# Sharing out the hidden layer of a relative-position bias anew, with the order of a head pair's steps changed

## The chip, the core and the metric

The kernel runs on one core of one Trainium2 chip. A core has TensorE (matrix products into the accumulator memory PSUM), VectorE, ScalarE and GpSimd (element work; GpSimd reads and writes only the core's main memory SBUF here) and SyncE, whose queue SP issues most DMAs. Each engine takes its instructions in order from a queue of its own and waits on semaphores for the others. The metric is the device time of one execution in microseconds (us), median over several runs.

## The reference

Attention with a learned bias of the relative position, then two gated feed-forward stages. Two batches, 8 heads, 576 positions, head size 64; the hidden layer of the bias has 32 units.

```python
scores = scale * np.matmul(q, k.transpose(0, 1, 3, 2))
psi_rel = np.log1p(np.abs(rel))                       # rel[i, j] = i - j
psi_i = np.log1p(np.maximum(pos[:, None], 1.0))
h = np.maximum((psi_rel / psi_i)[..., None] @ w1 + b1, 0.0)
scores = scores + (h @ w2).transpose(2, 0, 1)[None]   # one bias for both batches
attn = np.exp(scores - np.max(scores, axis=-1, keepdims=True))
attn = attn / (np.sum(attn, axis=-1, keepdims=True) + 1e-09)
x = np.matmul(attn, v)                                # then x @ w_a * (x @ w_b) @ w_out,
                                                      # and a softmax-gated, normed stage
```

## The kernel before

**The bias rows.** The bias of 16 query rows (one T; 576 / 16 = 36 of them) is made in three steps. `bias_hidden(T)` (line 348) makes four relus: for each quarter qd a tile h of 128 partitions (4 rows times 32 hidden units) by 576 positions, read as a shifted window of one table `tabs`, plus a column, then the maximum with 0. The division by psi_i is left until the end, which the maximum allows. Which engine makes each of the four is a string of `HIDDEN` (line 29): v is VectorE, p GpSimd (both line 365), a ScalarE (line 363). The strings are taken by T modulo their number, from the first tuple for the first 128 query rows (T = 0 to 7) and from the last for all others. `bias_sums(T)` (line 368) multiplies the four h by w2 on TensorE, 16 instructions (line 373) into four bands of one PSUM tile bps. `bias_out(T)` (line 376) copies bps, scaled, to a tile st with ScalarE (line 383) and sends st by DMA on SP into the rows of the bias (line 385).

**The prelude** (lines 514 to 535): T = 0 to 8. In step T come the relus of T, then sums and rows of T - 1, then the subtraction of one piece of turned queries or keys and the transposes and high copy of the next: a piece is transposed by TensorE (line 275), its rounded high part is copied by ScalarE (line 308) and the remainder is subtracted by VectorE (lines 313 and 317). Loads for the second query unit, the second batch's keys and the values are issued on SP behind the last rows.

**The loop** (lines 605 to 666) runs over 36 head pairs, 9 units of 128 query rows (`units`) by 4 pairs of heads, and three more steps that empty the pipeline. In step m:

- `scores` (line 389) of both heads of pair m; each head takes a PSUM tile from the pool `ps_s`, which has two buffers and also serves bps. The second head's buffer, `spare`, takes also the tails of the transposed shares of pair m - 2 (line 439) and four transposes of queries for the next unit (line 275).
- `biased` (line 405): VectorE adds the bias and takes the minimum of the (negated) scores in one pass for each head (line 415); `powers` (line 419): ScalarE's exponential with its sum (line 422).
- `kept_tails` and `high`: ScalarE copies tails (line 455) and the high part of the new queries (line 308) out of `spare`; `lower` (line 310): VectorE subtracts for the low part (line 317).
- `turned` (line 441): TensorE transposes the shares of pair m - 2 (line 450) into the one buffer of `ps_t`; `kept` (line 458) copies one half of the result with VectorE (r = 1) and one with ScalarE (r = 0) (line 464).
- `values` (line 466): shares of pair m - 3 times values, 40 small products on TensorE (line 482). At the last pair of a unit, `inputs_high` and `inputs_low` (lines 488 and 493) split the finished outputs with ScalarE and VectorE.
- In steps 0 to 26: `bias_sums` and `bias_out` of T = m + 9, and `bias_hidden` of T + 1 (before the change its VectorE relus come ahead of `lower`, the others at the end).
- `summed_powers` (line 424): GpSimd adds 1e-9 to the sums (line 427), VectorE takes the reciprocal (line 428); `shares` (line 430): GpSimd multiplies each head's exponentials by it (line 433).
- `others`: work for later stages (loads of values, and from step 27 on the first weights), keyed by twice the step. In steps 1 to 3 the second batch's keys are turned as pieces; in the last two pairs of a unit the queries of the unit after next are fetched on SP (line 256).

The text of the program is the order of every engine's queue: nothing is rearranged. Buffers of a pool are given to tiles when the program is built, and a tile's first writer waits for the readers of the tile that had its buffer.

**Behind the loop** come the feed-forward stages, bound by TensorE; they reuse the memory of the attention and begin when it ends.

Of the kernel before, what the change touches and what calls it, by code (L numbers as in the profile page):

```python
# [25 lines left out]

LAG = 2

HIDDEN = (("vpva", "vpvp"), ("vpvp",))

LOADS = ((0, 1), (1, 1), (2, 2), (3, 2))
FIRST = ((-7, -5, -3, 1, 2, 3), (-6, -4, -2, 3, 4, 5), (-5, 0, 2, 5, 6, 7), (2, 4, 5, 6, 8, 9))
# [18 lines left out]
def tile_kernel(ctx, tc, q, k, v, w1, b1, w2, w_a, w_b, w_out, w_in2, w_out2, g_ln, psi, rpsi, out):  # L51
# [19 lines left out]
    scale = 1.0 / math.sqrt(D)  # L71
# [88 lines left out]
    with ExitStack() as actx:  # L160
# [149 lines left out]
        def lower(views, by=1.0):  # L310
            for hi, lo, ps in views:
                if by == 1.0:
                    nc.vector.tensor_tensor(out=lo, in0=ps, in1=hi.bitcast(F32), op=ALU.subtract)
                    continue
                parts_ = [(lo, ps, hi)] if len(ps.shape) == 3 else [(lo[:, h], ps[:, h], hi[:, h]) for h in range(2)]
                for l_, p_, h_ in parts_:
                    nc.vector.scalar_tensor_tensor(out=l_, in0=p_, scalar=by, in1=h_.bitcast(F32), op0=ALU.mult, op1=ALU.subtract)
# [30 lines left out]
        def bias_hidden(T, engines="vpa"):  # L348

            it, r, c = place(T)  # L350
            kinds = HIDDEN[min(it, len(HIDDEN) - 1)]
            kinds = kinds[T % len(kinds)]
            hs = bias_w.setdefault(T, [None] * 4)
            for qd in range(4):
                e = kinds[qd]
                if e not in engines:
                    continue
                t0 = it * P + r + 16 * qd
                h = hp.tile([P, S], F32, tag="h", name=f"h_{T}_{qd}")
                win = tb[:, OFF - t0 - c:OFF - t0 - c + S]  # L360
                sc = nb[:, c, t0 // 16:t0 // 16 + 1]
                if e == "a":
                    nc.scalar.activation(h, win, AF.Relu, bias=sc)
                else:
                    (nc.vector if e == "v" else nc.gpsimd).tensor_scalar(h, win, sc, 0.0, op0=ALU.add, op1=ALU.max)  # L365
                hs[qd] = h
# [38 lines left out]
        def biased(u, h):  # L405

            it, _ = units[u]
            ps = st_.pop(("s", u, h))
            if h % 2 == 0:
                st_["e", u, h // 2] = ep.tile([P, 2 * S], F32, tag="e", name=f"e_{u}_{h}")  # L410
            e2 = st_["e", u, h // 2]
            e = e2[:, (h % 2) * S:(h % 2 + 1) * S]
            nm = sp.tile([P, 1], F32, tag="nm", name=f"nm_{u}_{h}")
            halves = lambda a: a.rearrange("p (a j) -> p a j", a=2)
            nc.vector.tensor_tensor_reduce(out=halves(e), in0=ps[:, :, 0:SH], in1=halves(bias_t[it][:, h, :]), op0=ALU.add, op1=ALU.min,  # L415
                                           scale=1.0, scalar=3.0e38, accum_out=nm)
            st_[u, h] = e, nm

        def powers(u, h):
            e, nm = st_[u, h]  # L420
            sums, _ = st_[u]
            nc.scalar.activation(e, e, AF.Exp, bias=nm, scale=-1.0, accum_out=sums[:, h:h + 1])  # L422

        def summed_powers(u, p):
            sums, rec = st_[u]
            heads = slice(2 * p, 2 * p + 2)
            nc.gpsimd.tensor_scalar(rec[:, heads], sums[:, heads], 1e-9, 1.0, op0=ALU.add, op1=ALU.mult)  # L427
            nc.vector.reciprocal(rec[:, heads], rec[:, heads])  # L428

        def shares(u, h):  # L430
            e, _ = st_.pop((u, h))
            _, rec = st_[u]
            nc.gpsimd.tensor_scalar(e, e, rec[:, h:h + 1], 1.0, op0=ALU.mult, op1=ALU.mult)  # L433
# [7 lines left out]
        def turned(u, p):  # L441

            e2 = st_.pop(("e", u, p))
            pt = ps_t.tile([P, 2, 512], F32, tag="t", name=f"pt_{u}_{p}")
            for j in range(2):
                for c in range(NC):
                    at = (j * NC + c) * HF
                    cols = j * S + j * TL + c * P
                    for r, rows in enumerate(ROWS):
                        nc.tensor.transpose(pt[:, r, at:at + HF], e2[rows, cols:cols + P], ident[rows, rows])  # L450
            st_["pt", u, p] = pt
# [6 lines left out]
        def kept(u, p, r):  # L458

            if r == 1:  # L460
                st_["et", u, p] = etp.tile([P, 2 * NC, P], F32, tag="et", name=f"et_{u}_{p}")
            dst = st_["et", u, p][:, :, ROWS[r]]
            pt = st_["pt", u, p][:, r].rearrange("p (c t) -> p c t", t=HF)
            (nc.vector.tensor_copy if r else nc.scalar.copy)(dst, pt)

        def values(u, p):

            it, bs = units[u]
            if p == 0:
                st_["x", u] = ps_x.tile([P, HP, P], F32, tag="x", name=f"px_{u}")  # L470
            px = st_["x", u]
            et, ett = st_.pop(("et", u, p)), st_.pop(("ett", u, p))
            n = P // len(bs)
            for c in range(NC + 1):
                for j, part in ((j, part) for j in range(2) for part in range(2)):

                    rows = slice(j * D + part * HID, j * D + (part + 1) * HID)
                    for m, b in enumerate(bs):
                        cols = slice(m * n, (m + 1) * n)
                        lhsT = (vsb[:, b, c] if c < NC else vtl[:, b])[:, p, j, part * HID:(part + 1) * HID]  # L480
                        rhs = et[:, j * NC + c, cols] if c < NC else ett[:, cols]
                        nc.tensor.matmul(px[rows, p, cols], lhsT, rhs, start=(c == 0 and m == 0), stop=(c == NC), skip_group_check=True)  # L482
# [14 lines left out]
        pairs = [(u, p) for u in range(NU) for p in range(HP)]  # L497
# [101 lines left out]
        def others(n):  # L599
            for f, args in extra.pop(n, []):  # L600
                f(*args)

        bias_hidden(sums_at[0])
        NP = len(pairs)
        for m in range(NP + LAG + 1):
            now = pairs[m] if m < NP else None
            up = pairs[m - LAG] if 0 <= m - LAG < NP else None
            out_ = pairs[m - LAG - 1] if 0 <= m - LAG - 1 < NP else None
            T, after = sums_at.get(m), sums_at.get(m + 1)
            views = []  # L610
            if now:
                u, p = now
                scores(u, 2 * p)
                spare = scores(u, 2 * p + 1)
                if (u, p) in ((NU - 3, HP - 1), (NU - 2, 1)):
                    clear_q(NU - 1, NU - 2 - u == 0)
            elif up:
                spare = ps_s.tile([P, 2, 512], F32, tag="s", name=f"tails_{m}")
            if up:
                turned_tails(*up, spare)  # L620
            if now and u + 1 < NU:
                g, i = divmod(p, 2)
                nat = fetched[("q", u + 1, g, 0)]
                turn(spare, QUERIES, nat, (2 * i, 2 * i + 1))
                views = q_views(u + 1, g, i, spare, QUERIES)
            if now:
                biased(u, 2 * p)
                powers(u, 2 * p)
                biased(u, 2 * p + 1)
            if up:  # L630
                kept_tails(*up, spare)
            high(views, -scale)
            if now:
                powers(u, 2 * p + 1)
            if up:
                turned(*up)
            if T is not None:
                bias_sums(T)
            if out_:
                values(*out_)  # L640
            if up:
                kept(*up, 1)
            others(2 * m)
            if after is not None:
                bias_hidden(after, "v")
            lower(views, -scale)
            if T is not None:
                bias_out(T)
            if up:
                kept(*up, 0)  # L650
            if after is not None:
                bias_hidden(after, "pa")
            for w in keys_at.get(m, []):
                made = piece(w)
                high(*made)
                lower(*made)
            if now:
                summed_powers(u, p)
                shares(u, 2 * p)
                shares(u, 2 * p + 1)  # L660
            if out_ and out_[1] == HP - 1:
                inputs_high(out_[0])
                inputs_low(out_[0])
            if now and p > 1 and u + 2 < NU:
                fetch(("q", u + 2, p - 2, 0))
            others(2 * m + 1)
# [155 lines left out]
    up = ctx.enter_context(tc.tile_pool(name="up", bufs=2))  # L822
# [117 lines left out]
    for i, u in enumerate(seq[:-2]):  # L940
        after = seq[i + 2]
# [66 lines left out]
```

## Time and profile before

| | us |
|---|---|
| median of 3 runs | 610.28 (608.60 to 612.89) |
| the profiled execution | 612.79 |
| its span, first to last instruction | 611.0 |
| prelude (first relu to first scores) | 6.3 to 41.6 |
| pairs 0 to 3 | 41.6 to 70.5 |
| pairs 4 to 26, with bias rows | 70.5 to 217.4 |
| pairs 27 on, to the end of the attention | 217.4 to 281.9 |
| feed-forward stages | 281.9 to 611.0 |

The profile is of one execution. Times in a row are us from the span's start; an instruction is named by its line, engine, operation and its tiles (output <- inputs, numbers left out). PE is TensorE, PEld its weight load, DVE is VectorE, ACT ScalarE, POOL GpSimd. In brackets stands how long the engine had been idle ahead of it and what ended that.

### The profile page before, as it was taken

Reading aid. Unit: us, or ns where it says so; the run is one execution under the profiler, and the core shown is the slowest. Engines: PE = TensorE matmul, PEld = TensorE weight load, DVE = VectorE, ACT = ScalarE, POOL = GpSimd, SP = SyncE. Lnnn points to the kernel's source line nnn. Section 1 sums busy time; section 2 is a strip of 40 time slices with the busy share of each in tenths; the row PEclk is TensorE's granted clock in tenths of the full one; section 3 lists DMA queues with packets and bytes.
Section 4 is the critical chain, followed back from the end, with each engine's and each line's share of the span. In section 5 each row is a group of like instructions: output and inputs, shape, how many; then the busy total and the mean of one; then the engine's idle time right before and its main releaser. Section 6 shows DMA issues by size and latency. Waiting matters only on the chain.

```text
span 611.0 us, 13442 instructions
## 1 busy us (share of the span) xinstructions
PE 527.6 (86%) x5416; PEld 458.6 (75%) x5416; DVE 396.5 (65%) x846; ACT 263.7 (43%) x584; POOL 288.4 (47%) x276
## 2 busy tenths in 40 slices
PE   7767766766667778889899999999999999999997
PEld 2324554555546667789899999999999998888887
DVE  4426646556556457753887998988988556675562
ACT  3425544545545456532555543444244432321221
POOL 6998899999999954410322221223412433000000
PEclk9996899899988989989899999999999999999999
DMA  5239733233132451104435443434531000000001
GB/s 134 77 88 192 165 75 77 58 77 75 46 88 59 114 142 59 38 1 138 141 112 165 138 138 121 151 111 137 160 115 36 2 0 1 18 35 18 17 18 52
DMA packets 63521, 51.75 MB, mean 85 GB/s; under 512 B 41182, under 2 KB 53731, under 8 KB 63460
## 3 DMA queue, kind: packets, MB, share of 16 engines
q1 hardware_dynamic: 63184, 50.88, 30.7%
q8 instruction: 42, 0.69, 0.5%
q14 instruction: 19, 0.16, 0.1%
q10 hardware_dynamic: 276, 0.02, 0.0%
HBM read 36.73 MB, written 2.36 MB: 64 GB/s over the span
## 4 chain that ended last, share of the span: by engine, by line
PE 60%; POOL 27%; issue 4%; DVE 3%; ACT 3%; DMA 3%; SPq 1%; POOLq 0%; DVEq 0%; ACTq 0%
PE pm L128 24%; POOL h L365 20%; PE po L128 12%; PE py L905 8%; PE ph L845 8%; POOL e L433 6%; PE bps L373 2%; PE px L482 1%; DMA nat_q<-in_q_dram 1%; PE pl L886 1%; ACT e L422 1%; PE s L401 1%; DMA words<-in_moe_w_out_dram 1%; POOL rec L427 1%; DVE e L415 1%
## 5 line engine op out<-in xcount | busy, mean ns | idle before, releaser
L365 POOL TENSOR_SCALAR h<-tabs 128x576 f32<-128x576 f32 x68 | 152.1, 2250 | 2.2 <-DVE tabs L216 2.2
L98 POOL TENSOR_SCALAR f<-f 128x512 f32<-128x512 f32 x48 | 41.3, 860 | 146.9 <-ACT f L94 140.2
L373 PE MATMUL bps<-h,w2bd 128*32 128x288 f32 x576 | 61.6, 459 | 46.8 <-DVE nm L415 39.2
L422 ACT ACTIVATE e<-e,nm 128x576 f32<-128x576 f32 x72 | 55.8, 775 | 91.8 <-DVE nm L415 90.3
L128 PE MATMUL pm<-xhi,abh 128*128 128x384 f32 x240 | 80.2, 334 | 0.0
L128 PE MATMUL pm<-xhi,abl 128*128 128x384 f32 x240 | 80.2, 334 | 0.0
L128 PE MATMUL pm<-xlo,abh 128*128 128x384 f32 x240 | 80.2, 334 | 0.0
L373 PEld LDWEIGHTS bps<-h,w2bd 128*32 128x32 f32 x576 | 22.6, 118 | 69.1 <-DVE nm L415 42.3
L415 DVE CUSTOM_DVE_ANT_0 e<-s,bias 128x576 f32<-128x576 f32 x72 | 51.9, 753 | 17.3 <-PE s L401 8.9
L433 POOL TENSOR_SCALAR e<-e,rec 128x576 f32<-128x576 f32 x72 | 55.2, 779 | 13.9 <-DVE rec L428 12.3
L128 PE MATMUL po<-gh,oh 128*128 128x384 f32 x144 | 48.5, 337 | 0.6 <-DVE x2s L776 0.6
L428 DVE RECIPROCAL rec<-rec 128x2 f32<-128x2 f32 x36 | 6.0, 166 | 65.8 <-POOL rec L427 65.5
L128 PE MATMUL po<-gh,ol 128*128 128x384 f32 x144 | 48.4, 336 | 0.0
L128 PE MATMUL po<-gl,oh 128*128 128x384 f32 x144 | 48.4, 336 | 0.0
L128 PEld LDWEIGHTS pm<-xhi,abl 128*128 128x128 f32 x240 | 45.1, 188 | 0.0
L128 PEld LDWEIGHTS pm<-xhi,abh 128*128 128x128 f32 x240 | 45.1, 188 | 0.0
L128 PEld LDWEIGHTS pm<-xlo,abh 128*128 128x128 f32 x240 | 45.1, 188 | 0.0
L872 POOL TENSOR_TENSOR small<-small,mhalf 128x1 f32<-128x1 f32 x9 | 5.0, 552 | 83.0 <-DVE small L871 49.4
L110 DVE SCALAR_TENSOR_TENSOR f<-words,f 128x512 int32<-128x512 int32 x48 | 42.5, 885 | 1.6
L482 PE MATMUL px<-et,vsb 128*32 128x128 f32 (+1 forms) x1280 | 43.5, 281 | 0.0
L482 PEld LDWEIGHTS px<-et,vsb 128*32 128x32 f32 x1280 | 37.4, 118 | 6.4 <-issue 1.5
L147 ACT COPY one<-pm 128x384 f32<-128x384 f32 x36 | 17.2, 477 | 56.7 <-PE pm L128 56.7
(149 smaller groups left out, 1282.6 us busy)
## 6 DMA issues: line engine op xcount, KB each, us to landing
bias<-st SPq DMA_DIRECT2D x40, 288.0 KB, 3.5
words<-in_moe_w_out_dram SPq DMA_DIRECT2D x20, 512.0 KB, 3.7
words<-in_moe_w_a_dram SPq DMA_DIRECT2D x12, 512.0 KB, 3.6
words<-in_moe_w_b_dram SPq DMA_DIRECT2D x12, 512.0 KB, 3.6
nat_q<-in_q_dram SPq DMA_DIRECT2D x32, 128.0 KB, 3.5
words<-in_moe_w_in_dram SPq DMA_DIRECT2D x8, 512.0 KB, 3.6
arena<-in_k_dram SPq DMA_DIRECT2D x16, 128.0 KB, 3.2
vsb<-in_v_dram SPq DMA_DIRECT2D x16, 128.0 KB, 2.8
```

The lines of the kernel that those rows point to most:

```text
L98: engine.tensor_scalar(f, f, WORD_MAX, WORD_MIN, op0=ALU.min, op1=ALU.max)
L110: nc.vector.scalar_tensor_tensor(out=b, in0=words[:, :, 0], scalar=29, in1=b, op0=ALU.logical_shift_right, op1=ALU.bitwise_or)
L128: nc.tensor.matmul(ps, w, x, start=(i == 0), stop=(i == n - 1))
L147: nc.scalar.copy(one, ps[:, 1])
L365: (nc.vector if e == "v" else nc.gpsimd).tensor_scalar(h, win, sc, 0.0, op0=ALU.add, op1=ALU.max)
L373: nc.tensor.matmul(bps[32 * qd:32 * qd + 32, a, 0:SH], w2bd, h[:, a * SH:(a + 1) * SH], start=True, stop=True)
L415: nc.vector.tensor_tensor_reduce(out=halves(e), in0=ps[:, :, 0:SH], in1=halves(bias_t[it][:, h, :]), op0=ALU.add, op1=ALU.min, scale=1.0, ...
L422: nc.scalar.activation(e, e, AF.Exp, bias=nm, scale=-1.0, accum_out=sums[:, h:h + 1])
L433: nc.gpsimd.tensor_scalar(e, e, rec[:, h:h + 1], 1.0, op0=ALU.mult, op1=ALU.mult)
L482: nc.tensor.matmul(px[rows, p, cols], lhsT, rhs, start=(c == 0 and m == 0), stop=(c == NC), skip_group_check=True)
L845: nc.tensor.matmul(ph[u][:, a], x[:, kc, cols], w[:, kc, a * 512:(a + 1) * 512], start=(i == 0), stop=(i == 3 * KD - 1))
L905: nc.tensor.matmul(ps, x[:, c, :], w[:, c, cols], start=(i == 0), stop=(i == 3 * KF - 1))
```

## The change

Three things. `HIDDEN` has one tuple of four strings for all T: of 16 relus 10 are VectorE's and 3 each ScalarE's and GpSimd's (before: 8 and 8 on VectorE and GpSimd in the loop; in the first 8 T, ScalarE also made one in every second T). The quarter that GpSimd makes is always the first. The sum, the reciprocal and the shares of a pair are issued one step later, the first two behind the next pair's `biased`, the shares behind its second `powers`. And within a step `values` comes ahead of `bias_sums`, both `kept` and `lower` ahead of `bias_hidden`, all of whose relus now stand together ahead of `bias_out`.

```diff
-HIDDEN = (("vpva", "vpvp"), ("vpvp",))
+HIDDEN = (("pvav", "vvav", "pvva", "pvvv"),)
...
         for m in range(NP + LAG + 1):
             now = pairs[m] if m < NP else None
+            last = pairs[m - 1] if 0 < m <= NP else None
...
                 biased(u, 2 * p)
                 powers(u, 2 * p)
                 biased(u, 2 * p + 1)
+            if last:
+                summed_powers(*last)
             if up:
                 kept_tails(*up, spare)
             high(views, -scale)
             if now:
                 powers(u, 2 * p + 1)
+            if last:
+                for h in range(2):
+                    shares(last[0], 2 * last[1] + h)
             if up:
                 turned(*up)
+            if out_:
+                values(*out_)
             if T is not None:
                 bias_sums(T)
-            if out_:
-                values(*out_)
             if up:
                 kept(*up, 1)
+                kept(*up, 0)
+            lower(views, -scale)
             others(2 * m)
             if after is not None:
-                bias_hidden(after, "v")
-            lower(views, -scale)
+                bias_hidden(after)
             if T is not None:
                 bias_out(T)
-            if up:
-                kept(*up, 0)
-            if after is not None:
-                bias_hidden(after, "pa")
             for w in keys_at.get(m, []):
                 made = piece(w)
                 high(*made)
                 lower(*made)
-            if now:
-                summed_powers(u, p)
-                shares(u, 2 * p)
-                shares(u, 2 * p + 1)
```

## Rows read from the trace of the kernel before

**Rows 1.** The page's chain that ended last: shares of the span by line

```profile
PE pm L128 24%; POOL h L365 20%; PE po L128 12%; PE py L905 8%; PE ph L845 8%; POOL e L433 6%; PE bps L373 2%; PE px L482 1%; DMA nat_q<-in_q_dram 1%; PE pl L886 1%; ACT e L422 1%; PE s L401 1%; DMA words<-in_moe_w_out_dram 1%; POOL rec L427 1%; DVE e L415 1%
```

**Rows 2.** By stage: us; busy PE, PEld, DVE, ACT, POOL (count); clock; DMA share; GB/s

```profile
6.30:41.60 35.30, 27.85 (x212) 11.48 (x212) 16.18 (x34) 12.29 (x22) 35.08 (x17) 1.00 0.40 100
41.60:70.50 28.90, 19.30 (x241) 13.36 (x242) 15.83 (x41) 14.73 (x33) 24.19 (x19) 0.76 0.82 175
70.50:217.40 146.90, 99.00 (x2080) 80.06 (x2076) 83.67 (x234) 75.21 (x189) 136.81 (x115) 0.95 0.34 77
217.40:281.90 64.50, 54.54 (x1089) 48.68 (x1088) 39.70 (x95) 32.92 (x86) 23.14 (x38) 0.92 0.19 52
```

**Rows 3.** The chain in order of time, one round of it: start, us, what

```profile
124.32 1.46 POOL e L433 x2
125.78 4.37 POOL h L365 x2
```

**Rows 4.** Timeline of TensorE: first scores of pair 4 and of pair 27

```profile
70.52 0.38 PE L401 MATMUL s<-khi,qhi 64*128 64x288 f32 x2
...
217.35 0.40 PE L401 MATMUL s<-khi,qhi 64*128 64x288 f32 x2
```

**Rows 5.** Waits from 70.5 to 217.4: us in total, times, longest

```profile
DVE rec L428 <- POOL rec L427: 61.2, 23, 2.8
...
PEld s L401 <- ACT st L383: 11.3, 15, 0.8
```

**Rows 6.** Durations, ns (minimum/median/maximum), by line; the last a mean in the loop

```profile
L365 DVE TENSOR_SCALAR h<-tabs x72: 501/514/1001, 6.3 to 210.5; 128x576 f32<-128x576 f32 x72
L365 POOL TENSOR_SCALAR h<-tabs x68: 2196/2208/2676, 6.4 to 211.7; 128x576 f32<-128x576 f32 x68
...
L363 ACT ACTIVATE h<-tabs x4: 775/776/783, 6.3 to 27.4; 128x576 f32<-128x576 f32 x4
...
L493 DVE TENSOR_TENSOR xlo<-px,xhi 128x512 fp32r<-128x512 f32 x5 | 3.4, 671 | 0.0
```

**Rows 7.** Timeline of the loop, pair 12 (scores from 121.75): start, us, instruction

```profile
125.00 1.20 PE L373 MATMUL bps<-h,w2bd 128*32 128x288 f32 x16 [1.51 <-DVE nm L415]
...
125.04 0.78 ACT L422 ACTIVATE e<-e,nm 128x576 f32<-128x576 f32 x1 [2.87 <-DVE nm L415]
...
126.14 1.10 DVE L365 TENSOR_SCALAR h<-tabs 128x576 f32<-128x576 f32 x2
...
127.00 0.73 ACT L383 ACTIVATE st<-bps,rp 128x576 f32<-128x576 f32 x1
127.62 0.59 ACT L464 COPY et<-pt 128x512 f32<-128x512 f32 x1
```

**Rows 8.** Timeline of a pair without bias rows and the next scores

```profile
228.18 0.40 PE L401 MATMUL s<-khi,qhi 64*128 64x288 f32 x2
...
228.68 0.29 PE L401 MATMUL s<-khi,qhi 64*128 64x288 f32 x2
...
229.13 0.29 PE L275 MATMUL s<-ident,nat_q 64*128 64x64 f32 x4
...
229.56 0.75 DVE L415 CUSTOM_DVE_ANT_0 e<-s,bias 128x576 f32<-128x576 f32 x1
229.69 0.78 ACT L422 ACTIVATE e<-e,nm 128x576 f32<-128x576 f32 x1 [1.79 <-DVE nm L415]
...
231.08 0.40 PE L401 MATMUL s<-khi,qhi 64*128 64x288 f32 x2
```

**Rows 9.** Prelude: key pieces' subtractions (count, busy us, mean ns); the last scaled copy

```profile
L313 DVE TENSOR_TENSOR klo<-tp_k,khi 128x512 fp32r<-128x512 f32 (+1 forms) x5 | 3.2, 638 | 6.4 <-ACT khi L308 6.4
...
41.80 0.74 ACT L383 ACTIVATE st<-bps,rp 128x576 f32<-128x576 f32 x1 [3.63 <-PE bps L373]
```

**Rows 10.** Timeline behind the prelude: query loads issued, and their first transposes

```profile
43.15 2.66 SPq L256 DMA_DIRECT2D nat_q<-in_q_dram  x4
...
47.63 0.48 PE L275 MATMUL s<-ident,nat_q 64*128 64x64 f32 x4 [4.37 <-DMA nat_q<-in_q_dram]
```

## The prediction

> **What bounds the kernel now.** I read the chain that ended last first. By line it gives 20% to the relus on GpSimd and 6% to its shares [rows 1]: a quarter of the time on an engine with no part in the matrix products. The busy times by stage show where [rows 2]. From 6.3 to 41.6 us (the prelude: bias rows T = 0 to 8) GpSimd is busy for 35.08 of 35.30 us, from 70.5 to 217.4 (23 head pairs that also make bias rows) for 136.81 of 146.90; no other engine passes 79% in the prelude or 68% in the loop. From 41.6 to 70.5 the DMA engines are the fullest resource (0.82), and from 217.4 on TensorE. The chain in order of time shows the loop's round: two shares 1.46, two relus 4.37, the sum and the reciprocal, and again [rows 3]. The second scores of a pair begin at 70.52 for pair 4 and at 217.35 for pair 27, by the first matmul of each [rows 4], so a round takes (217.35 - 70.52) / 23 = 6.384 us. The waits say how GpSimd stops the others: 23 times VectorE stands at the reciprocal until GpSimd has formed the sum, 61.2 us in all, with the next pair's bias-and-minimum queued behind it [rows 5].
>
> **The change part by part.** All sums are made against the profiled execution, 612.79 us; the median of the runs is 610.28, 2.5 lower, and the same gain is taken from it at the end.
>
> *Relus, engine by engine.* One relu is 0.514 on VectorE, 2.208 on GpSimd, 0.776 on ScalarE (medians [rows 6]). In the loop a pair now has 2 on VectorE and 2 on GpSimd; the new order of four has 2.5, 0.75 and 0.75. Busy per pair today is the loop's row over 23: TensorE 4.30, VectorE 3.64, ScalarE 3.27, GpSimd 5.95 [rows 2]. With the change GpSimd has 5.95 - 1.25 x 2.21 = 3.19, VectorE 3.64 + 0.5 x 0.51 = 3.90, ScalarE 3.27 + 0.75 x 0.78 = 3.85, TensorE 4.30. GpSimd falls from first to last, and no engine's sum can hold the loop above 4.30: that is the lower end of a round.
>
> *Sum, reciprocal and shares a pair later.* Nothing is added. The reciprocal stands behind this pair's two bias-and-minimum passes and waits for powers of the pair before, long done, and for GpSimd to be free of its relu. The first transposes that read the shares come one pair later than they are made, so they keep most of a round as cover; without it the wait would be at most the two shares, 1.46. VectorE's stall of 61.2 us goes, and what is late next is the order of the steps within a pair.
>
> *The new round.* What is late next is the ScalarE queue, whose scaled copy of the bias sums (st) frees a PSUM buffer that scores of the next pair take; today these scores wait for st 15 times [rows 5]. st now stands behind one copy of the transposed shares and, three times in four, a relu. If the buffer freed by st goes to the second head's scores, the round runs from st to st: scores and the transposes into the same buffer 0.74 (228.68 to 229.42), bias-and-minimum 0.75, and 0.2 for three hand-overs (an estimate from the 0.14 between 229.42 and 229.56) [rows 8]; on ScalarE 1.19 until st would have begun today (125.04 to 127.00, less 0.77 for the first exponential), then copy 0.49, relu 0.68, st 0.73, each starting 0.1 before the end of the last as at 127.62 [rows 7]; 0.06 to the scores: 4.84. Without a relu st waits for the bias sums: 2.40 (228.68 to 231.08, a pair without bias sums [rows 8]) + 1.20 for them [rows 7] + 0.06 + 0.73 = 4.40. Mean of three and one: 4.73. At every fourth pair VectorE's low half of the outputs (0.67 [rows 6]) waits for ScalarE and stands ahead of the two passes of the next pair; about 1.2, or 0.3 a round: 5.0. I take 5.1 for what semaphores add. The values, 1.2 us of TensorE, now stand ahead of the bias sums; these still end at 3.60, 0.4 before st can begin behind a relu, which is their cover, and each tenth beyond it would lengthen the round by as much. On SP the rows' DMA and the query loads behind it are issued 1.2 later in a pair, with st; the loads took 4.4 to land in the prelude (43.15 to 47.63 [rows 10], an issue among them) and are used two rounds, 10 us, later: nothing. Gain 23 x (6.384 - 5.1) = 29.5. Bounds: 4.30 gives 47.9; a round of 6.38, if something that I don't see holds it, gives 0.
>
> *Prelude.* Of the 40 relus for T = 0 to 9, GpSimd has 16 now and 7 then, VectorE 20 and 25, ScalarE 4 and 8. GpSimd: 35.08 - 8 x 2.21 = 17.4 (15 of its 16 lie in the stretch); VectorE 16.18 + 5 x 0.51 = 18.7; ScalarE 12.29 + 4 x 0.78 = 15.4; TensorE 27.85 as it runs now [rows 2], less then, since four bands of bias sums side by side take 1.20 [rows 7] and now they wait for GpSimd band by band. The stretch ends between 18.7 and 27.9; the key pieces are turned, copied and subtracted (0.64 each on VectorE [rows 9]) one at a time between the relus, which keeps it off the lower end. I take the middle, 23.3: gain 35.3 - 23.3 = 12.0, bounds 7.4 and 16.6. The last st ends at 42.54 now [rows 9]; the query loads are issued behind it and the first pair waits 4.37 for them [rows 10]; they move with it.
>
> *Pairs 0 to 3* are held by loads and by key pieces, which alternate between TensorE, ScalarE and VectorE, and stay as they are: 0, bounds 3 lost (the relu on ScalarE ahead of the pieces, 0.78 each, and st later) and 2 gained.
>
> *Pairs 27 to 38* have no relus. VectorE no longer waits at the reciprocal, and the second copy comes earlier on ScalarE; but TensorE is busy for 54.54 of 64.50 there [rows 2]. I take 1 gained, from 2 lost to 6 gained. Later stages hang on the end of this one and move with it.
>
> The sum: 12.0 + 29.5 + 0 + 1 = 42.5, so 570.3 on the profile's scale and 567.8, say 568, for the median.
>
> *A rule that speaks against it.* In the loop VectorE does two relus in 1.10 us, starting 0.36 after GpSimd began a pair of its own of 4.37 [rows 3, 7]: 0.07 more than twice the median, so neither waits for the other. The Trainium skill (SBUF — State Buffer, section Who interferes with whom) says that VectorE in a two-port mode, for which it names this form of operation, and GpSimd hold a shared pair of ports exclusively, the second blocking for a whole instruction. By that rule the change moves work onto the engine that is locked out, with the time of the last rival below; this trace disagrees with it for the relus, and no row shows relus on VectorE beside shares on GpSimd.
>
> **The rivals.** *The freed buffer goes to the first head's scores instead,* as 15 waits show it does mostly now [rows 5]. Then nothing of the next pair starts before st: from the scores to the first exponential 1.51 (228.18 to 229.69 [rows 8]) + 1.96 + 0.49 + 0.68 + 0.73 + 0.05 = 5.42, without a relu 4.93, mean 5.30, 0.15 for every fourth pair and 0.1 as above: 5.55. Gain 19.2 + 13 = 32.2: 578. For it: that is today's order. Against it: the subtractions that free the other buffer now come ahead of the relus, and st comes two steps later, so the other buffer is free first. *The prelude's gain is given back:* in pairs 0 to 3 the DMA engines are 0.82 busy [rows 2], and loads that arrive no earlier would keep the loop's start: 30.5 gained, 580. Against it: the loads are issued behind the last st and so move. *Better:* a round near TensorE's sum, 4.5, with 14 in the prelude and 3 at the end: 60 gained, 550. *Nothing reaches the end:* a round that stays near 6.3 by an order that I don't see, and a prelude with little: within 1%. *VectorE and GpSimd exclude each other* wherever both touch SBUF: a round is then their sum, 3.90 + 3.19 = 7.09, 16.2 lost over 23, and the prelude 18.7 + 17.4 = 36.1, 0.8 lost: 627 on the median's scale, 2.7% slower. It decides once over 2.5 of VectorE's 3.90 in a pair can't run beside GpSimd. Today's rows show 1.1 that can, hence the small chance.
>
> **How the numbers follow.** My forecast 0.55, with a range of its own of 560 to 575; first head's scores 0.22; prelude given back 0.09; better 0.07; within 1% 0.04; exclusion 0.03. One per cent, 6 us, is about what a measurement of this kernel can tell from no change. Faster by more than that: 0.55 + 0.22 + 0.09 + 0.07 = 0.93; same 0.04; slower 0.03. The range runs from 555 to 584: it holds the forecast, the two weaker gains and a part of the better one.
>
> **What would show it.** GpSimd under 60% busy in the loop; starts of scores about 5.1 apart, their waits on st moved to the second head's scores (5.55 and the first head's mean the first rival); the wait of the reciprocal for the sum gone; the last st of the prelude near 30 us; VectorE's relus still near 0.51. A round above 6, a prelude above 38 us, or relus of 0.8 and more on VectorE would make the prediction wrong.

## The result and the profile after

The changed kernel takes 570.56 us (median of 4 runs, 570.18 to 571.03); the kernel before, run beside it, 610.13 (608.60 to 612.89). The ratio is 0.935, 95% interval 0.931 to 0.938. The forecast was 568, in a range of 555 to 584; the medians differ by 39.6, where a gain of 42.5 was forecast. The profiled execution took 570.18 us with a span of 568.2.

By stage, with the columns of [rows 2]: us, busy time of each engine with its count of instructions, clock, share of the DMA engines, GB/s. The stages are those of before: the prelude, pairs 0 to 3, the loop with bias rows, pairs 27 on, the feed-forward stages.

```profile
6.40:30.60 24.20, 17.32 (x212) 8.13 (x212) 19.21 (x39) 14.83 (x25) 18.27 (x9) 0.93 0.54 133
30.60:59.16 28.56, 18.36 (x244) 12.59 (x242) 18.02 (x44) 16.43 (x37) 12.49 (x13) 0.82 0.85 187
59.16:176.26 117.10, 98.20 (x2079) 76.59 (x2074) 102.06 (x245) 88.19 (x206) 78.84 (x86) 0.99 0.42 97
176.26:241.56 65.30, 54.23 (x1091) 48.17 (x1088) 40.23 (x95) 33.21 (x86) 22.89 (x38) 0.92 0.19 52
241.56:568.20 326.64, 321.86 (x1752) 301.85 (x1752) 240.34 (x440) 126.56 (x252) 67.48 (x78) 1.00 0.27 85
```

Against [rows 2] the first scores come 11.0 us earlier (30.6 for 41.6), pairs 0 to 3 give 0.3, the loop 146.90 - 117.10 = 29.8, the pairs after it lose 0.8, and the feed-forward stages give 2.5: together 42.8, the difference of the spans (611.0 - 568.2). GpSimd, full before, is busy for 78.84 of 117.10 us of the loop, 67%; VectorE for 87%, TensorE for 84%. No engine is full: a chain across engines holds the round.

The chain that ended last, by line, names the parts of that chain. The relus of GpSimd, 20% in [rows 1], are no longer among the first fifteen lines; VectorE's bias-and-minimum (L415) rises from 1% to 4%, and its relus (L365), st (L383) and ScalarE's relu (L363) are among those that are new there:

```profile
PE pm L128 25%; PE po L128 13%; PE py L904 9%; PE ph L844 9%; DVE e L415 4%; DVE h L365 4%; ACT st L383 3%; PE s L401 2%; PE bps L373 2%; PE px L482 2%; ACT h L363 2%; DVE qlo L317 2%; ACT et L464 2%; ACT e L422 1%; PE pl L885 1%
```

The waits from 59 to 180 us (us in total, times, longest). VectorE's waits at the reciprocal, 61.2 us in [rows 5], are gone, and the scores' wait for st has grown from 15 times and 11.3 us to 24 times and 22.9:

```profile
POOL e L433 <- DVE rec L428: 38.0, 24, 4.3
PEld s L401 <- ACT st L383: 22.9, 24, 1.5
PE s L401 <- ACT st L383: 17.3, 23, 1.3
```

One round of the timeline (start, duration, instruction), from the second head's scores of one pair to those of the next. Follow the chain down: scores, their bias-and-minimum, the second exponential, the copy of the shares, the relu, st, and the next second scores, which begin as st ends. The first head's scores (93.98) wait for nothing:

```profile
90.45 0.40 PE L401 MATMUL s<-khi,qhi 64*128 64x288 f32 x2 [0.30 <-ACT st L383]
...
91.51 0.75 DVE L415 CUSTOM_DVE_ANT_0 e<-s,bias 128x576 f32<-128x576 f32 x1
...
92.87 0.77 ACT L422 ACTIVATE e<-e,nm 128x576 f32<-128x576 f32 x1
...
93.63 0.58 ACT L464 COPY et<-pt 128x512 f32<-128x512 f32 x1
...
93.98 0.40 PE L401 MATMUL s<-khi,qhi 64*128 64x288 f32 x2
94.10 0.79 ACT L363 ACTIVATE h<-tabs 128x576 f32<-128x576 f32 x1
...
94.78 0.74 ACT L383 ACTIVATE st<-bps,rp 128x576 f32<-128x576 f32 x1
...
95.57 0.41 PE L401 MATMUL s<-khi,qhi 64*128 64x288 f32 x2 [0.93 <-ACT st L383]
```

The round here is 95.57 - 90.45 = 5.12. Four rounds make a unit, and second heads that begin at 81.08, 85.96, 90.45, 95.57 and 101.38 us give 4.88, 4.49, 5.12 and 5.81, the last with the split of the finished outputs in it; the mean, by the first heads' scores, is 117.10 / 23 = 5.09, where 5.1 was forecast.

One forecast failed at once: the relus of VectorE. The durations by line, to be held against [rows 6]:

```profile
L365 DVE TENSOR_SCALAR h<-tabs x90: 501/792/1001, 6.4 to 172.7; 128x576 f32<-128x576 f32 x90
L365 POOL TENSOR_SCALAR h<-tabs x27: 2207/2404/2677, 6.5 to 171.6; 128x576 f32<-128x576 f32 x27
```

The median relu on VectorE is 0.79 us, not 0.51, and that on GpSimd 2.40, not 2.21. So the time was right, and two things wanted testing: which of the three edits earned it, and whether the slow relus cost anything.

### The profile page after: what moved, and what is told of

Its sections match the earlier page's. It is cut to its first block, busy times and chain, and to the rows that moved or that the text cites. A ratio compares the mean times of both kernels' runs of the same rounds, so it can differ in the third digit from the quotient of the medians.

```text
span 568.2 us, 13476 instructions
## 1 busy us (share of the span) xinstructions
PE 513.5 (90%) x5416; PEld 448.9 (79%) x5416; DVE 420.6 (74%) x864; ACT 281.4 (50%) x607; POOL 201.8 (36%) x235
## 4 chain that ended last, share of the span: by engine, by line
PE 67%; DVE 14%; ACT 10%; issue 4%; DMA 2%; SPq 1%; POOL 1%; DVEq 0%; ACTq 0%; POOLq 0%
PE pm L128 25%; PE po L128 13%; PE py L904 9%; PE ph L844 9%; DVE e L415 4%; DVE h L365 4%; ACT st L383 3%; PE s L401 2%; PE bps L373 2%; PE px L482 2%; ACT h L363 2%; DVE qlo L317 2%; ACT et L464 2%; ACT e L422 1%; PE pl L885 1%
## 5 line engine op out<-in xcount | busy, mean ns | idle before, releaser
L365 POOL TENSOR_SCALAR h<-tabs 128x576 f32<-128x576 f32 x27 | 64.9, 2406 | 8.2 <-PE bps L373 5.4
L415 DVE CUSTOM_DVE_ANT_0 e<-s,bias 128x576 f32<-128x576 f32 x72 | 52.6, 751 | 20.6 <-PE s L275 14.0
L365 DVE TENSOR_SCALAR h<-tabs 128x576 f32<-128x576 f32 x90 | 62.7, 745 | 2.8 <-PE bps L373 2.8
L373 PE MATMUL bps<-h,w2bd 128*32 128x288 f32 x576 | 47.2, 446 | 3.2 <-POOL h L365 3.1
L401 PE MATMUL s<-khi,qhi 64*128 64x288 f32 x128 | 26.0, 400 | 20.8 <-ACT st L383 17.9
L401 PEld LDWEIGHTS s<-khi,qhi 64*128 64x128 f32 x128 | 12.6, 190 | 40.6 <-ACT st L383 24.6
L482 PE MATMUL px<-et,vsb 128*32 128x128 f32 (+1 forms) x1280 | 41.5, 275 | 0.0
L94 ACT ACTIVATE f<-words 128x512 f32<-128x512 f32 x48 | 32.4, 676 | 17.9 <-DMA words<-in_moe_w_out_dram 6.9
```

Source lines behind the costliest of these rows:

```text
L373: nc.tensor.matmul(bps[32 * qd:32 * qd + 32, a, 0:SH], w2bd, h[:, a * SH:(a + 1) * SH], start=True, stop=True)
L401: nc.tensor.matmul(ps[:, a, 0:SH], w[r], x[r, b, h, :], start=(i == 0), stop=(i == len(mm) - 1))
```

## Experiments

A round in what follows is the start of the second bias-and-minimum of pair 27 less that of pair 4, divided by 23: 6.38 before (220.14 less 73.32), 5.10 after (178.97 less 61.61). Ratios are to the kernel before in the same batch.

| kernel | us | ratio (95%) | round |
|---|---|---|---|
| the change | 570.6 | 0.935 (0.931 to 0.938) | 5.10 |
| e1: old order, new relus | 558.9 | 0.917 (0.914 to 0.921) | 4.66 |
| e2: new order, old relus | 613.3 | 1.007 (1.004 to 1.010) | 6.51 |
| e3: change, sums and shares in their own step | 571.0 | 0.937 (0.934 to 0.940) | 5.10 |
| e4: change, values behind the bias sums | 570.0 | 0.935 (0.932 to 0.938) | 5.05 |
| e5: change, st ahead of the relus | 564.3 | 0.925 (0.922 to 0.928) | 4.80 |
| e12: e5 and e3 together | 564.7 | 0.925 (0.921 to 0.930) | 4.80 |
| e13: e12, second copy behind st | 564.3 | 0.924 (0.921 to 0.928) | 4.81 |
| e14: e13, values behind the bias sums | 559.5 | 0.917 (0.914 to 0.921) | 4.71 |
| e9: e1, second copy and relus ahead of st | 569.6 | 0.935 (0.931 to 0.939) | 5.07 |
| e10: e1, low half of the outputs later | 549.1 | 0.900 (0.897 to 0.903) | 4.33 |
| e11: e5, low half of the outputs later | 556.2 | 0.912 (0.909 to 0.915) | 4.59 |

**The relus or the order.** First each half of the change alone. The kernel before with the new sharing out of the relus only:

```diff
-HIDDEN = (("vpva", "vpvp"), ("vpvp",))
+HIDDEN = (("pvav", "vvav", "pvva", "pvvv"),)
```

> The kernel before with the new sharing of the relus alone; order of the steps as before, so the buffer freed by the scaled copy goes mostly to the first head's scores. Theory A (the relus carry the gain, GpSimd was the bound): GpSimd's sum per pair falls from 5.95 to 3.2 us, the scaled copy has no relu ahead of it, and a round is set by scores 1.51, ScalarE 1.96, copy 0.73 and VectorE's relus ahead of the subtraction, 4.6 to 5.2 us instead of 6.38; prelude as in the changed kernel, last scaled copy near 31.6; time 560 to 575. Theory B (without the later sums VectorE still stands at the reciprocal behind GpSimd's relu): the wait of the reciprocal for the sum stays above 1 us a pair, a round is 5.5 or more, time 580 to 590.

And the changed kernel with the old sharing out:

```diff
-HIDDEN = (("pvav", "vvav", "pvva", "pvvv"),)
+HIDDEN = (("vpva", "vpvp"), ("vpvp",))
```

> The changed kernel with the old sharing of the relus: the order alone. Theory A: GpSimd still has a sum 0.19, two shares 1.46 and two relus 4.4 in each pair, 6.05 us, and now waits only for a reciprocal; a round is 6.1 to 6.4, the prelude as before (last scaled copy near 42.5), time 600 to 612. Theory B (the order carries the gain): a round under 5.6 and a time of 580 to 592.

The relus alone bring 610 to 558.9, 11.7 us under the whole change; the order alone makes the kernel 0.7% slower. So the relus earn the whole gain, and in their company the order takes part of it back. Each time the first theory held in kind, though both times lie 1 us outside its range (560 to 575, 600 to 612), and e2's round of 6.51 outside 6.1 to 6.4. The profiled spans, 568.2 and 556.1, say where: of 12.1 us, 1.1 lie ahead of pair 4, 10.1 in the 23 rounds (117.36 for 107.24), 1.3 behind them, less 0.4 in the feed-forward stages. In e1 the reciprocal, though not moved, hardly waits any more (waits from 59 to 160 us):

```profile
DVE rec L428 <- POOL rec L427: 6.1, 12, 0.6
```

That was 61.2 us in [rows 5]: the stall that the lag was to remove goes with GpSimd's load. And the timeline of e1 shows st straight behind the second exponential, which began at 89.38, and the relu behind both st and the copy:

```profile
90.05 0.20 ACT L422 ACTIVATION_READ_ACCUMULATOR e<-e,nm 128x1 f32 x1
90.14 0.74 ACT L383 ACTIVATE st<-bps,rp 128x576 f32<-128x576 f32 x1
...
90.76 0.59 ACT L464 COPY et<-pt 128x512 f32<-128x512 f32 x1
...
90.93 0.40 PE L401 MATMUL s<-khi,qhi 64*128 64x288 f32 x2 [0.17 <-ACT st L383]
...
91.23 0.80 ACT L363 ACTIVATE h<-tabs 128x576 f32<-128x576 f32 x1
```

In the changed kernel 94.78 - 92.87 = 1.91 us lie between the starts of the second exponential and of st; here 90.14 - 89.38 = 0.76.

In e2 the slower relu on GpSimd is enough for the loss in the rounds. From 70 to 160 us 28 relus there have a mean of 2.304, in the kernel before 29 have 2.226; 46 relus of the loop times 0.078 are 3.6 us. The 23 rounds of the profiled executions differ by 2.9 (149.7 for 146.8), and the ratio of 1.007 is 4.2. No run changes this alone, so it is argued and not shown. The row of e2:

```profile
L365 POOL TENSOR_SCALAR h<-tabs 128x576 f32<-128x576 f32 x28 | 64.2, 2304 | 0.0
```

**Two parts of the order undone alone.** The changed kernel with sum, reciprocal and shares back at the end of their own step:

```diff
-            if last:
-                summed_powers(*last)
...
-            if last:
-                for h in range(2):
-                    shares(last[0], 2 * last[1] + h)
...
+            if now:
+                summed_powers(u, p)
+                shares(u, 2 * p)
+                shares(u, 2 * p + 1)
```

> The changed kernel with sum, reciprocal and shares back at the end of the same pair's step. Theory A: the round goes from the scaled copy through the second head's scores, minimum, exponential, copy and relu; the sum is ready about 3.1 us after the second scores begin, the reciprocal 0.3 later, and the next minimum is due at about 4.2, so nothing is late: round 5.0 to 5.2, time 568 to 574. Theory B: VectorE is held at the reciprocal and the next minimum starts later, 0.3 us or more a pair, time 577 or more.

And the changed kernel with `values` behind `bias_sums` again:

```diff
-            if out_:
-                values(*out_)
             if T is not None:
                 bias_sums(T)
+            if out_:
+                values(*out_)
```

> The changed kernel with the values behind the bias sums again. Theory A: the bias sums end 1.2 us earlier in a round, which only a round without a relu on ScalarE can use (4.48 us now, perhaps 4.2 then), and nothing else waits for the values: 0 to 2 us gained, time 568 to 571. Theory B (the values fill a gap in which TensorE waited for relus): the sums wait for GpSimd's or VectorE's last relu with the values behind them, 0.2 us or more a pair, time 575 or more.

Neither moves the time (571.0 and 570.0). In e3 VectorE's relus are back at a median of 0.512 and the round is still 5.10:

```profile
L365 DVE TENSOR_SCALAR h<-tabs x90: 500/512/1028, 6.3 to 173.2; 128x576 f32<-128x576 f32 x90
```

So the lag and the slow relus that come with it cost next to nothing together in this order; e3 undoes both, and can't price either alone. The mean hides a little: in e3 two rounds took 6.53 from the first bias-and-minimum of a pair to that of the next, and in the changed kernel one took 6.35, each with 3.4 us in it at a granted clock of 0.50, which is 1.2 GHz (in the changed kernel from 122.1 to 125.5); all other rounds of these two loops had 1.00, 2.4 GHz. A unit without such a round takes 20.05 in e3 and 20.29 in the changed kernel, 0.06 a round. In e4 no round is slow, and its units take 20.30: its 5.05 for 5.10 is that one round. What is left of the order is the place of st.

**The place of st, from both sides.** The changed kernel with st ahead of the relus:

```diff
-            if after is not None:
-                bias_hidden(after)
             if T is not None:
                 bias_out(T)
+            if after is not None:
+                bias_hidden(after)
```

> The changed kernel with one line moved: the copy out of the bias sums (st) stands ahead of the four relus again, still behind both copies of the transposed shares. Theory A: what the new order costs is the relu on ScalarE ahead of st, three times in four 0.7 us on the chain st, second head's scores, its exponential, st. Then a round goes from 5.09 to 5.09 - 0.75 x 0.7 = 4.56, and the time from 570.6 by 23 x 0.53 = 12 to about 558. Rival B: VectorE sets the round, because its relus are held while GpSimd makes the shares (0.79 instead of 0.51 us): VectorE is busy 78.67 of 90 us, 4.45 of a round of 5.09, and the round stays between 4.9 and 5.1: 566 to 571.

And e1 with the second copy and the relus of ScalarE and GpSimd moved ahead of st:

```diff
-            if T is not None:
-                bias_out(T)
             if up:
                 kept(*up, 0)
             if after is not None:
                 bias_hidden(after, "pa")
+            if T is not None:
+                bias_out(T)
```

> The kernel before with the new shares of the relus (the run of 559), and of the new order only this: the second copy of the transposed shares and all relus of ScalarE and GpSimd stand ahead of the copy out (st). Sums and shares stay at the end of their own step, the values behind the bias sums. Theory A: st is late by the copy and the relu, the round goes from 4.64 to 5.0 to 5.2, and the time to 567 to 572, as in the changed kernel. Rival B (the lag of the sums, or shares beside VectorE's relus, are what costs): this kernel has neither, and stays within 3 us of 559.

The second is clear: 569.6, the time of the whole change, from one call moved down. Its timeline (e9) has the chain of the changed kernel again, with copy and relu between the exponential and st:

```profile
93.09 0.77 ACT L422 ACTIVATE e<-e,nm 128x576 f32<-128x576 f32 x1
...
93.85 0.57 ACT L464 COPY et<-pt 128x512 f32<-128x512 f32 x1
...
94.32 0.79 ACT L363 ACTIVATE h<-tabs 128x576 f32<-128x576 f32 x1
...
95.00 0.73 ACT L383 ACTIVATE st<-bps,rp 128x576 f32<-128x576 f32 x1
...
95.78 0.40 PE L401 MATMUL s<-khi,qhi 64*128 64x288 f32 x2 [0.64 <-ACT st L383]
```

The first met neither number: 564.3, half of what I expected. The relu was on the chain, but something else came up when 6 us were gained.

**What comes up next.** I took it for VectorE's slow relus, and undid the lag as well (the diffs of e5 and e3 together):

> Both moves at once: the changed kernel with the copy out ahead of the relus (alone 564) and with sum, reciprocal and shares back at the end of their own step (alone 571, no gain). Theory: two limits stand side by side. With the copy out early, VectorE is next, because its relus are held while GpSimd makes the shares (in that run every fourth round, 4.85 us, is the one with three relus on VectorE, 2.22 us for three instead of 1.54). With the shares away from them the relus are 0.51 again, that round falls to about 4.4, and the time to 557 to 561, where the run with the old order lies. Rival: the lag of the sums is worth nothing here either: 564, and the rest of the difference comes from the second copy of the transposed shares, which still stands ahead of the copy out.

That theory fell: 564.7. The relus are fast (median 0.515), and over the four rounds of a unit nothing changes: from the first bias-and-minimum of a pair to that of the next, 4.42 + 4.68 + 6.19 + 3.95 = 19.24 us, against 4.43 + 4.84 + 5.80 + 4.16 = 19.23 in e5. Why the last round of a unit grew by 0.39 I did not follow up. But the timeline of e12 shows what st waits for now:

```profile
107.26 0.78 ACT L422 ACTIVATE e<-e,nm 128x576 f32<-128x576 f32 x1
...
107.47 1.19 PE L373 MATMUL bps<-h,w2bd 128*32 128x288 f32 x16
...
108.02 0.58 ACT L464 COPY et<-pt 128x512 f32<-128x512 f32 x1
...
108.77 0.74 ACT L383 ACTIVATE st<-bps,rp 128x576 f32<-128x576 f32 x1 [0.17 <-PE bps L373]
```

The bias sums end at 108.66, later than the copy. They stand behind the values, so two things, the copy and the sums, hold st to nearly the same moment. I removed them one after the other: first the second copy goes behind st, then the values behind the bias sums.

```diff
             if up:
                 kept(*up, 1)
-                kept(*up, 0)
...
             if T is not None:
                 bias_out(T)
+            if up:
+                kept(*up, 0)
             if after is not None:
```

> The run of 564.7 (copy out ahead of the relus; sum, reciprocal and shares in their own step) with the second copy of the transposed shares behind the copy out as well, so that the copy out follows the second exponential at once. Theory: little is won, since in that run 8 of 19 copies out already begin behind the end of the bias sums (waits of 0.17 us), which come 1.2 us later than before because the values stand ahead of them: the bias sums then hold the copy out, 562 to 565. Rival: the second copy was all that was left, 0.6 of each chain from copy out to copy out, of which a quarter shows: 558 to 560.

```diff
-            if out_:
-                values(*out_)
             if T is not None:
                 bias_sums(T)
+            if out_:
+                values(*out_)
```

> The run just above with the values behind the bias sums again. Nothing then holds the copy out: the second exponential ends, it begins. Theory (everything that the new order put ahead of the copy out costs, each as far as the others leave it uncovered): 557 to 561, the time of the kernel before with the new shares of the relus alone. Rival: the rest lies in which buffer the copy out frees (here always that of the second head's scores, in the run of 559 mostly that of the first head's), then it stays at 562 to 565.

Moving the copy does nothing (564.3): st now waits 0.43 for the sums. Moving the values then gives 4.8 us, 559.5, and e1's time is back. In its text e14 differs from e1 only in that VectorE's relus stand behind `lower`, so this last part of the order costs nothing to speak of (559.5 for 558.9). What the copy costs alone is not shown: no run has the values late and only the copy ahead of st. The timeline of e13, bias sums, second exponential and st:

```profile
89.06 1.19 PE L373 MATMUL bps<-h,w2bd 128*32 128x288 f32 x16
89.07 0.77 ACT L422 ACTIVATE e<-e,nm 128x576 f32<-128x576 f32 x1
...
90.36 0.74 ACT L383 ACTIVATE st<-bps,rp 128x576 f32<-128x576 f32 x1 [0.43 <-PE bps L373]
```

The same three in e14, where the sums end (90.91) before the exponential does:

```profile
89.71 1.20 PE L373 MATMUL bps<-h,w2bd 128*32 128x288 f32 x16 [0.53 <-DVE nm L415]
...
90.86 0.77 ACT L422 ACTIVATE e<-e,nm 128x576 f32<-128x576 f32 x1
...
91.61 0.74 ACT L383 ACTIVATE st<-bps,rp 128x576 f32<-128x576 f32 x1
```

The same edit was worth nothing in e4, where the relu stood behind it on the same path. The two profiled executions are 6.1 us apart: 2.3 lie in the 23 rounds (110.56 for 108.22), 2.6 ahead of pair 4 and 1.1 behind pair 27, where one execution of each doesn't settle it.

**Better than both.** From first scores to first scores the longest rounds of e1 are the last of each unit, 5.81 against 4.14 to 4.40 for the others from pair 5 on. Its timeline there says why: VectorE's low half waits for ScalarE's high half, which waits for the relu, and the next pair's bias-and-minimum stands behind:

```profile
91.91 0.60 ACT L488 CAST xhi<-px 128x512 fp32r<-128x512 f32 x1
92.54 0.69 DVE L493 TENSOR_TENSOR xlo<-px,xhi 128x512 fp32r<-128x512 f32 x1 [1.10 <-ACT xhi L488]
93.15 0.75 DVE L415 CUSTOM_DVE_ANT_0 e<-s,bias 128x576 f32<-128x576 f32 x1
```

So the low half was issued one step later, ahead of `summed_powers` in e1, and behind the relus in e5:

```diff
+            if gone is not None:
+                inputs_low(gone)
+                gone = None
             if now:
                 summed_powers(u, p)
...
                 inputs_high(out_[0])
-                inputs_low(out_[0])
+                gone = out_[0]
...
+        inputs_low(gone)
```

> The run of 559 (old order, new shares of the relus) with VectorE's low half of a finished unit's outputs issued one step later, behind the step's other VectorE work, so that the next pair's bias-and-minimum no longer waits behind it for ScalarE's high half. A round at the end of a unit takes 5.81 there, the others 4.16 to 4.39. Theory: the six unit ends of the loop lose about 1.4 us each and the three outside it 1 each: 559 - 11 = 548. Rival: the next thing late is ScalarE, which makes a relu and the high half ahead of the next exponentials, and half is given back: 553.

> The changed kernel with the copy out ahead of the relus, and the low half of a finished unit's outputs one step later. If theory A and the cost of the unit ends both hold: 558 less 9 (a unit's last round is 5.80 instead of 4.88 in the changed kernel, six times, and three more outside the loop), 549. If VectorE sets the round: 560 or more.

e10 takes 549.1, 10% under the kernel before and 3.8% under the change; as forecast for it (548); its rounds from pair 4 to 26 lie between 4.31 and 4.43. In its timeline at the end of a unit the bias-and-minimum now runs while ScalarE still makes the high half, and the low half finds it done:

```profile
90.61 0.76 DVE L415 CUSTOM_DVE_ANT_0 e<-s,bias 128x576 f32<-128x576 f32 x1
...
90.88 0.60 ACT L488 CAST xhi<-px 128x512 fp32r<-128x512 f32 x1
...
94.26 0.68 DVE L493 TENSOR_TENSOR xlo<-px,xhi 128x512 fp32r<-128x512 f32 x1
```

The same edit on e5 gave 8.1 (556.2), between the two numbers expected (549, and 560 or more), and 7 above e10: what e5 keeps of the order still costs that much.

## Why the prediction was right, step by step

- *GpSimd bounds prelude and loop; the relus free it.* Right, and shown by e1 and e2: all of the gain is the relus'. Its own sign, GpSimd under 60% busy in the loop, missed: 67%, and 3.19 of 5.1, its own sum, is 63%.
- *Busy per pair in the loop.* TensorE 98.20 / 23 = 4.27 (forecast 4.30), ScalarE 3.83 (3.85), GpSimd 3.43 (3.19), VectorE 4.44 (3.90). The last two failed mostly on one term, the duration of a relu beside the other engine: 0.79 for 0.51 and 2.40 for 2.21. That explains nearly all of VectorE's difference and about half of GpSimd's. I named 0.8 as the sign that would make the prediction wrong; at 0.79 it all but came. The round hung on st and not on VectorE's sum, and e3, with fast relus, has the same time. The 1.10 us of two relus in [rows 7], taken for no exclusion, were 0.67 and 0.51: the first was held, and where it falls in GpSimd's instruction decides for how long (last section).
- *The round, from st to st.* 5.09 measured, 5.1 forecast. With a relu 4.84 was forecast for 4.88 and 5.12, without one 4.40 for 4.49, at the end of a unit 6.0 (4.84 and 1.2) for 5.81, and every second head waits for st, as said. The step from 5.0 to 5.1 was an allowance with no row behind it; that it fits so well is luck in part. One reading in it is wrong: 70.52 and 217.35 are the first head's scores, as [rows 4] says; the second head's begin at 71.00 and 217.91, which gives 6.39 for 6.384 and changes nothing.
- *The first rival* (the freed buffer to the first head's scores, 578) did not come. Its price for a late st stays untested, and for its 4.93 without a relu the prediction shows no working. With an early st it makes no difference which head waits: in e1 the first head's scores begin as st ends (90.93, above), in e14 the second head's do (111.25 in its timeline, behind an st from 110.43 to 111.17), and both take 559.
- *The step that failed* is the account of the order's parts. I priced the lag at a gain (the stall of 61.2 us "goes") and the rest at nothing beside the round, and never worked out the round of the new relus in the old order. The stall goes with the relus alone. And I put the copy, 0.49, and the relu, 0.68, ahead of st in my own sum without asking what the round is with them behind it: 4.84 less these is 3.67, under TensorE's 4.30. The order costs 11.7 us, and one call moved (e9) 10.7 of them, which a sum over both halves could not show. So the time of both halves together was forecast rightly, and the belief that the order adds to the gain was wrong.
- *Values ahead of the bias sums: covered by 0.4.* Right in the changed kernel (e4: nothing); with the relu and the copy out of the way it costs 4.8 us (e13 to e14).
- *Prelude.* 11.0 gained, 12.0 forecast. The last st begins at 30.88 (forecast "near 30"); the stretch is 24.2 for 23.3. GpSimd was busy for 18.27 (17.4), VectorE for 19.21 (18.7), TensorE for 17.32, less than today's 27.85 as argued.
- *Pairs 0 to 3*: 0.3, forecast 0. *Pairs 27 on*: 0.8 lost, forecast 1 gained, inside its bounds.
- *Feed-forward stages*: 2.5 gained, forecast 0. This belongs to the one execution of before, where the granted clock was 0.50 from 292.9 to 296.3; in the changed kernel it was 1.00 all through. From the last low half to the end it takes 327.5 us there, and between 324.8 and 325.9 in all of the other traces measured so (e2, with the old relus, 324.9). Without it the profiled gain is 40.3, near the 39.6 of the medians; the sum of 42.5 was 2 to 3 us too high, 1.8 of it behind the loop and 1.0 in the prelude.

## What to carry to other kernels

When a change shifts work off the engine that bounds and reorders the queues as well, work out the round for the shift alone: the reorder may be undoing part of it. A copy that frees a buffer for the next round belongs straight behind the last thing it needs, ahead of any work that only has to be done some time in the round. Where two things hold an instruction to nearly the same moment, undoing one can look free; undo them together, or read off the timeline which one is left.

## What the runs showed that I had not expected

VectorE's relus and GpSimd's work do exclude each other, for a part of the time. Over all thirteen traces, by where in an instruction of GpSimd a relu on VectorE began ("in": us behind its start; "left": us ahead of its end):

| GpSimd's instruction | VectorE's relu began | relus | median us |
|---|---|---|---|
| none | | 257 | 0.51 |
| share (0.745 us) | 0.09 to 0.20 in | 76 | 0.94 |
| share | 0.20 to 0.27 in | 44 | 0.79 |
| share | 0.06 left | 5 | 0.53 |
| relu (2.2 to 2.7 us) | with it | 10 | 0.52 |
| relu | 0.24 to 0.30 in | 137 | 0.99 |
| relu | 0.30 to 0.48 in | 60 | 0.73 |
| relu | over 0.5 in, over 1.0 left | 326 | 0.51 |
| relu | 0.53 to 0.72 left | 97 | 0.92 |
| relu | under 0.3 left | 21 | 0.52 |

A VectorE relu that starts in a share ends 0.31 us after the share (the five with 0.06 left, 0.47), as if held until then. One that starts 0.24 to 0.48 us into a GpSimd relu is held too, but ends 1.2 to 1.4 us ahead of that relu's end; one that starts 0.53 to 0.72 us ahead of the end is held to 0.31 us after it; and one that starts between these stretches is not held at all, though GpSimd is still at work. So a GpSimd relu holds VectorE near its beginning and near its end, and lets it through in the middle. Three examples of one GpSimd relu and two of VectorE in a row: in the changed kernel the first begins in a share and the second near the relu's beginning (1.86 us for both), in e12 the second begins near its end (1.38), in e14 both begin in its middle (0.94):

```profile
84.42 2.40 POOL L365 TENSOR_SCALAR h<-tabs 128x576 f32<-128x576 f32 x1
83.81 1.86 DVE L365 TENSOR_SCALAR h<-tabs 128x576 f32<-128x576 f32 x2
...
82.92 2.20 POOL L365 TENSOR_SCALAR h<-tabs 128x576 f32<-128x576 f32 x1
84.06 1.38 DVE L365 TENSOR_SCALAR h<-tabs 128x576 f32<-128x576 f32 x2
...
81.46 2.34 POOL L365 TENSOR_SCALAR h<-tabs 128x576 f32<-128x576 f32 x1
82.34 0.94 DVE L365 TENSOR_SCALAR h<-tabs 128x576 f32<-128x576 f32 x2
```

In the loop of the kernel before, VectorE's relus began 0.38 to 1.35 us into GpSimd's, where they lost 0.16 us at most (0.67 at 0.38), and so [rows 7] showed no exclusion; the new order put them beside the shares and the beginning of a relu. The Trainium skill (SBUF — State Buffer, section Who interferes with whom) has the second of the two wait for the whole instruction of the first. For the shares the traces agree (0.79 to 0.94 beside a share of 0.745); for GpSimd's relus they do not, since 326 relus in the middle of one took 0.51. Where VectorE has slack the cost doesn't show in the time (e3, e12); where GpSimd has none (e2), the working above puts it at about 3.6 us, since GpSimd's relu loses too: 2.41 with a single VectorE relu in it begun about 0.3 us in (56 of them), 2.21 with VectorE idle (38).
